# Weight preparation and early attention steps placed anew in a fused RetNet and leaky-ReLU kernel

## The chip, the cores and the metric

The kernel runs on one core of a Trainium2 chip. The metric is the device time of one execution in microseconds (us). The span of a trace, from the first to the last instruction, is about 2 us shorter than the time of the same execution. The granted clock is the share of TensorE's full clock that the profile shows. PE is TensorE, PEld its weight load, DVE is VectorE, ACT ScalarE, POOL GpSimd.

## The reference, cut to what matters

```python
# B, H, S, D = 4, 8, 768, 64
for t in range(S):
    state = gamma[None, :, None, None] * state + np.einsum('bhd,bhe->bhde', k[:, :, t], v[:, :, t])
    y[:, :, t] = scale * np.einsum('bhd,bhde->bhe', q[:, :, t], state)
x = y.transpose(0, 2, 1, 3).reshape(B * S, H * D)     # 3072 x 512
h = x @ w_in                                          # w_in 512 x 2048
g = np.maximum(0.01 * h, h)
return (g @ w_out).astype(np.float32)                 # w_out 2048 x 512
```

The data is fp32; the two weights are float64, so their eight-byte words reach the chip and are rounded to fp32 there.

## The kernel before

The sequence is cut into six chunks of 128 positions, c = 0 to 5. A chunk needs four **attention steps**, one for each batch entry b. A step is scores (`stage_a`: TensorE into two PSUM banks, VectorE multiplies by the mask), then the reading of scores and state (`yp`), an eviction into `x`, and the state update (`sp`). Two loops over the hidden dimension follow, in four units u of 512. The two matrix products of a unit are done by a scheme with seven products instead of eight, M1 to M7. I name one round of the seven a **call**: h(c,u) for the hidden layer, o(c,u) for the output.

```python
def seven(tiles, name, takes):
    which = [("M1", "A", 0, 0), ("M6", "B", 5, 5), ("M5", "C", 4, 4), ("M4", "D", 3, 6),
             ("M2", "A", 2, 2), ("M7", "B", 1, 1), ("M3", "C", 6, 3)]
    ...        # 4 matmuls each (8 records in the trace); PSUM bank A, B, C or D, tag "ff", 6 banks in all
        takes(m, ps)          # VectorE or ScalarE evicts and adds
        yield
```

The order matters for waits: M7 takes the bank that M6 filled, so M7 cannot start before VectorE has read M6 (into `u2`, in the trace `u`). M3 takes the bank of M5 in the same way (`m5`, in the trace `m`).

The weights come as 32 **pieces**, four for each of the eight blocks win[0..3] and wout[0..3]. One call of `round_piece` does this:

```python
def round_piece():
    n = done[0]; done[0] += 1
    if n == N_PIECES - 4:
        last.extend(work.tile(..., tag="raw", bufs=3, name=f"last{h}") for h in range(3))
    round_words(n)              # 3 ACTIVATEs on ScalarE (power of two of each word),
                                # then 3 operations on VectorE (mantissa, times power)
    ...                         # load of a later piece: three buffers "raw",
                                # and ONE buffer "raw_end" for the last four pieces
    if n % 4 == 3:
        sums(units[n // 4])     # 4 VectorE operations once a block is complete
```

Below, **powers** are the three ScalarE operations, **mantissas** the three VectorE operations, and **differences** are four VectorE operations on `x` (or `g`, giving `gd`) that play for activations the part that sums play for weights. The schedule of the first two chunks was this; steps inside a call are counted from 0, so `rounds(2, 4)` rounds one piece after the third product and one after the fifth:

```python
units = [win[0], wout[0], win[1], wout[1], win[2], win[3], wout[2], wout[3]]
for b in range(B):                       # chunk 0
    scored(0, b)(); round_piece(); read(0, b)()
differences(*xs[0])
run(hidden(0, *part[:1], *xs[0], *part[1:]), **rounds(2, 4))
for b in range(B):                       # chunk 1
    scored(1, b)()
    if b % 2 == 0:
        round_piece()
    read(1, b)()
differences(*xs[1])
for u in range(NU // 2):                 # units 0 and 1, each for both chunks
    for c in range(2):
        ...                              # hidden, rounds(2, 4)
    for c in range(2):
        run(output(c, os[c], [parts[c]], u == 0, False), **rounds(1, 3, 5))
for c in range(2):                       # units 2 and 3 as a pair, one output call for both
    ...
```

## Time and profile before

| | before |
|---|---|
| time, median (lowest to highest) | 735.77 us (734.89 to 736.97), 3 runs |
| span of the trace, mean granted clock | 734.1 us, 0.980 |
| TensorE busy / VectorE busy | 689.7 us (94%) / 365.1 us (50%) |
| VectorE operations | 579 |

The whole document uses one division of the span. It needs three lines of TensorE's timeline: the first product M1 of chunk 0, of chunk 1 and of chunk 2. The columns are start in us, duration, engine, source line, operation, tiles, shape and count.

```profile
28.08 1.99 PE L273 MATMUL A_h<-x,win 128*128 128x256 f32 x8
...
78.83 1.99 PE L273 MATMUL A_h<-x,win 128*128 128x256 f32 x8
...
297.01 1.89 PE L273 MATMUL A_h<-x,win 128*128 128x256 f32 x8
```

They cut the 734.1 us into an **opening** of 28.08, a **first stage** of 50.75 (one hidden call of chunk 0 and the attention of chunk 1), a **second stage** of 218.18 (the other 15 calls of the first two chunks with the rounding of 24 of the 32 pieces, and the attention of chunk 2) and a **rest** of 437.09 (chunks 2 to 5). The change rewrites the first three.

### The profile page before, as it was taken

Reading aid. Unit: us, or ns where it says so; the run is one execution under the profiler, and the core shown is the slowest. Engines: PE = TensorE matmul, PEld = TensorE weight load, DVE = VectorE, ACT = ScalarE, POOL = GpSimd, SP = SyncE. Lnnn points to the kernel's source line nnn. Section 1 sums busy time; section 2 is a strip of 40 time slices with the busy share of each in tenths; the row PEclk is TensorE's granted clock in tenths of the full one; section 3 lists DMA queues with packets and bytes.
Section 4 is the critical chain, followed back from the end, with each engine's and each line's share of the span. In section 5 each row is a group of like instructions: output and inputs, shape, how many; then the busy total and the mean of one; then the engine's idle time right before and its main releaser. Section 6 shows DMA issues by size and latency. Waiting matters only on the chain.

```text
span 734.1 us, 9584 instructions
## 1 busy us (share of the span) xinstructions
PE 689.7 (94%) x4096; PEld 594.2 (81%) x4096; DVE 365.1 (50%) x579; ACT 164.0 (22%) x273; POOL 26.2 (4%) x29
## 2 busy tenths in 40 slices
PE   5667999989779999999999999999999999999997
PEld 5556888877658888888888888888888888888886
DVE  4857598899654354351355253255243246251342
ACT  4050265463510120021011011111021021031210
POOL 1201100000000010000000000000000000000000
PEclk9888999999979999999999999999999999999999
DMA  8716223231202310220020120021121000100001
GB/s 303 256 58 225 92 94 137 86 104 68 87 0 100 131 58 14 81 78 1 29 87 1 61 92 21 0 80 36 58 65 51 0 2 0 58 1 0 2 1 58
DMA packets 15163, 49.12 MB, mean 67 GB/s; under 512 B 1680, under 2 KB 1680, under 8 KB 15120
## 3 DMA queue, kind: packets, MB, share of 16 engines
q1 hardware_dynamic: 15120, 48.51, 19.0%
q8 instruction: 32, 0.52, 0.3%
q14 instruction: 11, 0.09, 0.0%
HBM read 42.21 MB, written 6.29 MB: 66 GB/s over the span
## 4 chain that ended last, share of the span: by engine, by line
PE 83%; DVE 11%; ACT 2%; issue 2%; DMA 1%; SPq 0%; DVEq 0%
PE B_o L273 11%; PE B_h L273 11%; PE C_o L273 10%; PE C_h L273 10%; PE A_h L273 10%; PE A_o L273 10%; PE D_o L273 5%; PE D_h L273 5%; PE yp L147 3%; PE yp L142 3%; PE a0p L123 3%; DMA raw<-in_weights_dram 1%; PE sp L158 1%; ACT g L288 1%; PE a1p L123 1%
## 5 line engine op out<-in xcount | busy, mean ns | idle before, releaser
L273 PE MATMUL A_h<-x,win 128*128 128x256 f32 x384 | 91.2, 380 | 1.1 <-ACT m L293 1.1
L273 PEld LDWEIGHTS A_h<-x,win 128*128 128x128 f32 x384 | 72.5, 190 | 11.4 <-ACT m L293 1.5
L273 PE MATMUL A_o<-g,wout 128*128 128x256 f32 x288 | 69.8, 383 | 0.0
L288 ACT ACTIVATE g<-g 128x512 f32<-128x512 f32 x72 | 43.9, 630 | 105.3 <-DVE g L238 105.3
L273 PEld LDWEIGHTS A_o<-g,wout 128*128 128x128 f32 x288 | 55.1, 192 | 8.0 <-ACT m L330 0.4
L152 DVE TENSOR_TENSOR x<-yp,dec 128x512 f32<-128x512 f32 x24 | 16.6, 690 | 86.6 <-PE yp L147 86.6
L293 ACT COPY m<-A_h 128x512 f32<-128x512 f32 x24 | 14.0, 584 | 199.3 <-PE A_h L273 191.3
L273 PE MATMUL B_h<-t,win 128*128 128x256 f32 x192 | 47.6, 392 | 4.8 <-DVE t L241 4.8
L273 PE MATMUL B_h<-x,win 128*128 128x256 f32 x192 | 46.7, 386 | 0.9 <-DVE u L238 0.9
L273 PE MATMUL C_h<-t,win 128*128 128x256 f32 x192 | 47.4, 390 | 0.0
L273 PEld LDWEIGHTS B_h<-t,win 128*128 128x128 f32 x192 | 37.2, 196 | 11.0 <-DVE t L241 5.6
L273 PE MATMUL C_h<-x,win 128*128 128x256 f32 x192 | 45.4, 379 | 0.0
L273 PE MATMUL D_h<-t,win 128*128 128x256 f32 x192 | 45.4, 379 | 0.0
L112 POOL TENSOR_TENSOR kv<-kv,dec 128x512 f32<-128x512 f32 x24 | 25.7, 1072 | 528.6 <-DMA kv<-in_kv_dram 481.7
L238 DVE TENSOR_TENSOR m<-m,B_o 128x512 f32<-128x512 f32 x14 | 9.6, 685 | 68.8 <-PE B_o L273 68.8
L123 PE MATMUL a0p<-qk 64*128 64x128 f32 x192 | 31.3, 307 | 11.1 <-DVE x L152 6.4
L273 PEld LDWEIGHTS C_h<-t,win 128*128 128x128 f32 x192 | 36.2, 193 | 6.1
L273 PEld LDWEIGHTS B_h<-x,win 128*128 128x128 f32 x192 | 35.4, 190 | 6.8 <-DVE u L238 1.3
L273 PEld LDWEIGHTS C_h<-x,win 128*128 128x128 f32 x192 | 36.5, 190 | 5.0
L273 PEld LDWEIGHTS D_h<-t,win 128*128 128x128 f32 x192 | 36.5, 190 | 5.0
L123 PEld LDWEIGHTS a0p<-qk 64*128 64x128 f32 x192 | 26.1, 205 | 17.7 <-DVE x L152 7.0
L273 PE MATMUL C_o<-g,wout 128*128 128x256 f32 x144 | 34.7, 381 | 2.8 <-DVE m L238 2.8
(91 smaller groups left out, 1077.8 us busy)
## 6 DMA issues: line engine op xcount, KB each, us to landing
raw<-in_weights_dram SPq DMA_DIRECT2D x32, 512.0 KB, 3.2
qk<-in_qk_dram SPq DMA_DIRECT2D x24, 512.0 KB, 3.8
kv<-in_kv_dram SPq DMA_DIRECT2D x24, 512.0 KB, 4.4
out_dram<-o SPq DMA_DIRECT2D x24, 256.0 KB, 2.0
dec<-decay_dram SPq DMA_DIRECT2D x1, 262.0 KB, 5.4
```

What stands on the lines that cost most here:

```text
L112: nc.gpsimd.tensor_tensor(out=v, in0=v, in1=gk.unsqueeze(2).to_broadcast([128, H, D]), op=ALU.mult)
L123: nc.tensor.matmul(ps[j][:, a, :], lhsT=x[ts(j, 64), 1, a, :], rhs=x[ts(j, 64), 0, a, :])
L142: nc.tensor.matmul(yp[ts(j, 64), a, :], lhsT=st[b][ts(j, 64), a, :], rhs=x[ts(j, 64), 0, a, :], start=(a == 0), stop=False, skip_group_che ...
L147: nc.tensor.matmul(yp[ts(j, 64), a, :], lhsT=vs[:, 2 * a + j, :], rhs=am[j][:, a, :], start=(c == 0 and a == 0), stop=True, skip_group_che ...
L152: nc.vector.tensor_tensor(out=blocks, in0=yp.rearrange("p (kh k) t -> p kh k t", k=2), in1=gq.rearrange("p (kh k) t -> p kh k t", k=2), op ...
L158: nc.tensor.matmul(sp[ts(j, 64), a, :], lhsT=ks[:, 2 * a + j, :], rhs=vs[:, 2 * a + j, :], start=(a == 0), stop=True, skip_group_check=True)
L238: nc.vector.tensor_tensor(out=out, in0=a, in1=b, op=ALU.add)
L273: nc.tensor.matmul(ps[:, i, :], lhsT=block(w, sa)[:, k, ts(i, 128)], rhs=rhs[:, k, :], start=(first and i == 0 and n == 0 and k == 0), sto ...
L288: nc.scalar.activation(g[:, i], g[:, i], AF.Prelu, alpha=0.01)
L293: nc.scalar.copy(out=got["m1"], in_=ps)
```

## The change

The intent is to take away waits of TensorE for VectorE and ScalarE before chunk 2:

1. All four units go through the first two chunks one at a time, in the order win[0], wout[0], win[1], wout[1] and so on, so each block is needed when it arrives. There is no pair of units any more, which costs two more partial output calls.
2. ScalarE's powers run two pieces ahead of VectorE's mantissas.
3. The last four pieces lie in the four buffers of the attention inputs instead of in a single one.
4. Scores of chunk 0 and of steps 2 and 3 of chunk 1 use the six PSUM banks of the products.
5. Steps 0 and 1 of chunk 1 are woven into the first hidden call, whose products get another order.
6. The sums of win[0] alternate with the differences of chunk 0 instead of going before the last eviction of `x`.
7. In hidden calls rounding moves from steps 2 and 4 to 1 and 3, in output calls from 1, 3 and 5 to 1 and 4.

The diff, cut to its core (cuts are marked with `...`; the rest makes generators of `sums` and `differences`, and adapts helpers and the host's order of the pieces):

```diff
-    def stage_a(c, b):
+    def stage_a(c, b, banks="att"):
-        ps = [psum.tile([128, HP, C], FP32, tag="att", bufs=2, name=f"a{j}p_{c}_{b}")
+        ps = [psum.tile([128, HP, C], FP32, tag=banks, bufs=BANKS[banks], name=f"a{j}p_{c}_{b}")
...
-        if n < NC * B:
+        if n < NC * B and n - 2 * B not in range(AHEAD):
             load(*divmod(n, B))
...
-    units = [win[0], wout[0], win[1], wout[1], win[2], win[3], wout[2], wout[3]]
+    units = [w for pair in zip(win, wout) for w in pair]
...
-        raws[n] = work.tile([128, W], I64, tag="raw_end" if end else "raw", bufs=1 if end else 3,
-                            name=f"raw{n}")
+        tag, bufs = ("raw", 3) if n < N_PIECES - 4 else (("qk", "kv")[n % 2], AHEAD)
+        raws[n] = work.tile([128, W], I64, tag=tag, bufs=bufs, name=f"raw{n}")
...
-            round_words(n)
+            mantissas(n)
+        load_piece(n + 3)
+        if n + 2 < N_PIECES and f64:
+            powers(n + 2)
...
+        if n % 4 == 3 and n > 3:
+            all_of(sums(units[n // 4]))
...
-        scored(0, b)()
+        scored(0, b, banks="ff")()
         round_piece()
         read(0, b)()
-    differences(*xs[0])
+    all_of(differences(*xs[0]), sums(win[0]))
...
+    for u in range(NU):
+        parts = []
         for c in range(2):
+            parts.append(new_g(c, u))
+            order = {}
+            at = rounds(1, 3)
+            if (c, u) == (0, 0):
+                xs[1] = new_x(1)
+                order["order"] = ("M1", "M2", "M6", "M5", "M4", "M7", "M3")
+                at = put(rounds(1), s0=[scored(1, 0)], s2=[read(1, 0)], s3=[scored(1, 1)],
+                         s5=[read(1, 1)])
+            elif (c, u) == (1, 0):
+                for b in range(2, B):
+                    scored(1, b, banks="ff")()
+                    round_piece()
+                    read(1, b)()
+                differ(1)()
+                at = rounds(1)
+            elif (c, u) == (1, NU - 1) and NC > 2:
+                xs[2] = new_x(2)
+                at = put(at, s4=[scored(2, 0)], s6=[read(2, 0)])
+            run(hidden(c, u, *xs[c], *parts[c][1:], **order), at)
         for c in range(2):
...
+            at = rounds(1, 4) if u < NU - 1 else {}
+            if u == NU - 1 and NC > 2:
+                if c == 0:
+                    at = dict([(0, [scored(2, 1)]), (2, [read(2, 1)]), (3, [scored(2, 2)]),
+                               (5, [read(2, 2)])])
+                else:
+                    at = {0: [scored(2, 3)], 2: [read(2, 3)], 4: [differ(2)]}
+            run(output(c, os[c], [parts[c]], u == 0, u == NU - 1), at)
```

## The prediction

> **What bounds the kernel now.** I read the page first (strips and chain), then a table of stretches, then TensorE's timeline where it has gaps. From the page:
>
> ```profile
> PE   5667999989779999999999999999999999999997
> DVE  4857598899654354351355253255243246251342
> PEclk9888999999979999999999999999999999999999
> ...
> PE 83%; DVE 11%; ACT 2%; issue 2%; DMA 1%; SPq 0%; DVEq 0%
> ```
>
> A slice is 18.4 us. TensorE is full from the 13th slice on (220 us) to the last but one. Only the time before has room: TensorE is at 5 to 7 tenths in the first four slices and at 7 in the 11th and 12th, after VectorE ran at 8 or 9 for five slices, and the granted clock dips. The 11% of VectorE in the chain (some 80 us) must therefore lie there too. The table of stretches sizes it (stretch, its length, then busy us and counts by engine, clock, DMA share, GB/s):
>
> ```profile
> 0.00:28.00 28.00, 17.60 (x192) 15.35 (x192) 14.87 (x27) 8.90 (x13) 4.66 (x9) 1.00 0.86 306
> 28.00:79.00 51.00, 34.96 (x316) 29.77 (x315) 34.56 (x54) 10.87 (x18) 5.93 (x5) 0.83 0.40 139
> 79.00:147.00 68.00, 67.48 (x312) 58.94 (x312) 54.30 (x89) 37.12 (x63) 1.04 (x1) 1.00 0.31 107
> 147.00:205.00 58.00, 50.02 (x228) 41.37 (x227) 47.42 (x79) 29.08 (x49) 0.00 (x0) 0.97 0.23 82
> 205.00:241.00 36.00, 30.58 (x210) 25.48 (x209) 17.52 (x29) 1.10 (x2) 1.04 (x1) 0.91 0.17 59
> 297.00:410.00 113.00, 113.00 (x707) 97.70 (x706) 46.60 (x75) 17.30 (x29) 4.17 (x4) 1.00 0.14 48
> ```
>
> Idle TensorE: 10.4 us, 16.0, 0.5, 8.0 and 5.4 in the first five, 0 in the sixth. The timeline names what ended the longest gaps:
>
> ```profile
> 34.37 3.78 PE L273 MATMUL B_h<-t,win 128*128 128x256 f32 x8 [4.29 <-DVE t L241]
> ...
> 54.48 1.97 PE L142 MATMUL yp<-qk,st 64*64 64x128 f32 x16 [5.90 <-DVE am L128]
> ...
> 150.10 1.99 PE L273 MATMUL B_o<-g,wout 128*128 128x256 f32 x8 [0.92 <-DVE u L238]
> ...
> 167.29 1.99 PE L273 MATMUL C_o<-g,wout 128*128 128x256 f32 x8 [1.65 <-DVE m L238]
> ...
> 199.08 1.34 PE L273 MATMUL A_o<-g,last 128*128 128x256 f32 x4 [2.23 <-ACT g L303]
> ...
> 211.19 2.07 PE L273 MATMUL B_o<-gd,last 128*128 128x256 f32 x4 [5.42 <-DVE gd L241]
> ```
>
> Each is TensorE waiting for VectorE, or for ScalarE held up by a weight piece that arrived late. After the first gap eight matmuls took 3.78 us where they take 1.73 elsewhere: the clock was halved.
>
> **What the Trainium skill says.** "TensorE: Matmul & The Clock Gate", Back-to-back issue gap: N/2.4 + 2.5 ns when warm, 109 ns at N = 256. The trace has eight records of 216 ns for one fp32 product of eight (1.727 us), so it agrees if each fp32 matmul runs two passes per record. The same page, What's actually happening: about 3.4 us of idling halves the clock and about 3.4 us of work restores it. The trace agrees for the gaps of 4.29 and 5.42 us. "VectorE: DVE Perf Modes", The perf-mode tier table: fp32 tensor_tensor has only the 1x mode; the errata section of that page gives (N+151)/0.96, or 691 ns at 512. The trace has 681 to 692 ns, and starts 0.60 us apart when independent, 0.72 when the second reads the first. "Perfetto Trace Analysis", Matmuls: independent groups should rotate through different PSUM banks so that eviction overlaps. That is the intent of moving the early scores; the trace shows the wait it removes (scores of head group 1 started 1.21 us late, behind the x eviction of group 0).
>
> **The change part by part.** Dense costs first. A "call" (seven products of one unit) is 7 x 1.727 = 12.09 us of TensorE. One chunk in steady state, from the first product at 297.01 to the next chunk's at 409.69, is 112.68 us for eight calls (96.7), so an attention step costs (112.68 - 96.7)/4 = 4.0 us.
>
> *Opening, to the first product (28.08 us before).* Scores in six other banks let scores b+1 follow directly on step b; powers made early take ScalarE's part (three ACTIVATEs, 1.93 us) out of VectorE's waits. But the K/V tiles of steps 2 and 3 were waited for by GpSimd until 19.64 and 24.31 us, with DMA at 0.86. I move those by under 1 us, so the first product starts at about 27.8: gain nearly 0.
>
> *From the first product to the second chunk's first (28.08 to 78.83 us before, 50.75 us).* Dense it is one call and four attention steps: 12.1 + 16 = 28.1. Walking the new order with the 0.60 and 0.72 us spacings: the eight interleaved differences and sums end at about 33.0 (36.5 before); M1, scores, M2 fill TensorE until 32.3, when M6's operands are ready; two attention steps lie between products, so M3 ends at about 47.5. Then the second half of chunk 1 starts as badly as before: VectorE finishes g and gd at 51.9 and the score masks at 53.1, so TensorE idles about 4 us and probably halves its clock. Two steps of some 4 us follow; chunk 1's first product comes at about 61.5. Interval 33.7 instead of 50.75: gain 17. One weight piece and one set of sums (1.87 + 2.6 us of VectorE) is left over to the next stage.
>
> *From there to chunk 2's first product (78.83 to 297.01 before, 218.2 us).* Fifteen calls and four attention steps: 15 x 12.09 + 16 = 197.3 dense; the kernel before loses 20.9 here. What the change adds: outputs one unit at a time, so two more partial outputs, 2 x 9 VectorE operations, 18 x 0.69 = 12.4 us. Is VectorE enough? Per unit (two hidden and two output calls, 48.4 us of TensorE): hidden 2 x 6.5 (nine operations and a 0.7 us wait for ScalarE), output 2 x 5.9, eight pieces x 1.87 (0.46 + 0.80 + 0.61 from start to start), two sums x 2.6: 13 + 11.8 + 15 + 5.2 = 45.0. It fits, at 93%. Lags inside: rounds move from steps 2 and 4 to 1 and 3 and no longer wait for ScalarE, so the first operation of the output call ends at 6 us into it (9.9 before, at 149.36), where M7 needs it at 8.6; its m5 at 9.0, where M3 needs it at 10.4. So the waits of 0.92 to 1.65 us vanish, narrowly. The last pieces no longer share one buffer but use the chunk-input buffers: the 2.23 and 5.42 us gaps vanish, with their half clock. New: in the last unit scores of step 1 share two banks with step 0, whose eviction follows gd; I find TensorE waiting about 2 us there, and 0.5 at chunk 1's first differences, 2.5 and 0.5 with some clock. Gain 20.9 - 3.0 = 17.9.
>
> *After chunk 2's first product*: the same code, 436.9 us, gain 0.
>
> Sum: 0 + 17 + 17.9 = 35 us. 735.8 - 35 = 701.
>
> **Rivals.** (1) VectorE becomes the bound in the first two chunks. For: 93% by my count, and the trace has operations of 762 to 932 ns on average in some groups of sums, and waits for ScalarE's leaky step of 0.7 us each; before, it was 82% busy in 147 to 205 and already stalled TensorE. Against: 79 to 147 ran at 80% with 0.5 us lost. If each of three units overruns by 4 us, 713. (2) Opening and chunk 1 stay bound by arrivals and by the mask-evict-mask chain with the clock halved. For: the GpSimd waits at 19.64 and 24.31. Against: after 28 us the DMA share is 0.40. Half the 17 us would be lost: 709. (3) Powers placed ahead of evictions on ScalarE block them when a piece is late. For: in-order engine, waits up to 6.3 us for raw pieces at the start. Against: three buffers, 3.2 us to landing against some 6 us between rounds, and ScalarE needs 24 of 48.4 us per unit. Worth up to 5 us. (4) On the other side, no half clock in chunk 1 and a shorter wait there: about 696.
>
> **Range and chances.** Rivals 1 to 3 add, each unlikely in full, and together weigh more than rival 4; the floor with no stall in either part is 735.8 - 22.6 - 20.9 = 692. Range 692 to 712. Faster by 2% means under 721, which needs less than half the sum: 0.95. Within 2%: 0.04. Slower: 0.01.
>
> **What would show it.** Right: first product still near 28 us; chunk 1's first product near 61.5; chunk 2's near 262; no idle TensorE over 1 us between 62 and 240; VectorE above 90% there; a gap of about 4 us near 50 and one of 2 us in the last unit; about 437 us afterwards. Wrong: gaps of 1 us or more before M7 or M3 of output calls (rival 1); chunk 1's first product after 68 (rival 2); ScalarE waiting for raw pieces just before a gap (rival 3); any change after chunk 2's first product.

## The result, and the profile after

| | before | after |
|---|---|---|
| time, median (lowest to highest) | 735.80 us (734.89 to 736.97), 4 runs | 703.74 us (702.56 to 705.67), 4 runs |
| span of the trace, mean granted clock | 734.1 us, 0.980 | 701.8 us, 0.987 |

The ratio is 0.9566 with a 95% interval of 0.954 to 0.9592: faster by 4.3%. Here and below a ratio is the mean time of one kernel's fast runs over the mean of the other's in the same group of runs, so it is not quite the ratio of the medians. The predicted time was 701, the range 692 to 712.

The page of the kernel after, first the totals, then the strips and the chain of the work that ended last (a slice is 17.5 us):

```profile
PE 680.5 (97%) x4096; PEld 589.9 (84%) x4096; DVE 373.5 (53%) x597; ACT 166.9 (24%) x275; POOL 26.6 (4%) x29
...
PE   4898999999999999999999999999999999999997
...
DVE  4868767888889555512553442544351354341442
...
PEclk9799999999999999999999999999999999999999
...
PE 92%; DVE 4%; DMA 2%; ACT 1%; issue 0%; POOL 0%; SPq 0%; DVEq 0%; POOLq 0%
```

TensorE now reads 8 or 9 from the second slice to the last but one, and VectorE's share of the chain fell from 11% to 4%. VectorE has 597 operations instead of 579: 18 more, and still less of the time hangs on it. Its digits stay at 7 to 9 from the seventh slice to the 13th, so it is not idle; it is in time. The table of stretches, at the new boundaries, with the second stage split by unit (length, then busy us and counts of PE, PEld, DVE, ACT, POOL, then clock, DMA share, GB/s):

```profile
0.00:28.70 28.70, 17.79 (x193) 15.88 (x193) 15.94 (x28) 12.78 (x19) 5.74 (x10) 0.82 0.83 308
28.70:62.20 33.50, 29.88 (x314) 25.00 (x312) 25.89 (x45) 9.23 (x15) 3.86 (x4) 0.95 0.39 138
62.20:99.80 37.60, 36.57 (x171) 31.91 (x169) 29.07 (x49) 17.66 (x29) 0.00 (x0) 1.00 0.26 84
99.80:148.20 48.40, 48.40 (x226) 42.67 (x225) 38.84 (x64) 23.23 (x38) 0.00 (x0) 1.00 0.24 78
148.20:196.50 48.30, 48.30 (x226) 42.59 (x225) 41.92 (x69) 22.90 (x38) 0.00 (x0) 1.00 0.31 108
196.50:264.40 67.90, 66.47 (x482) 56.40 (x481) 48.55 (x79) 11.94 (x20) 6.54 (x6) 0.97 0.34 113
```

Units 1 and 2 (99.8 to 196.5) take 48.4 and 48.3 us with TensorE busy in all of it; four calls of 12.09 us make 48.4. In the kernel before, TensorE idled for 8 us in the stretch from 147 to 205 us, which holds the output calls of unit 1 and the hidden calls of units 2 and 3 of chunk 0. TensorE's timeline has these boundaries and these gaps (the number in brackets is the idle time just before, with what ended it):

```profile
17.27 0.37 PE L125 MATMUL a0p<-qk 64*128 64x128 f32 x1 [2.03 <-DMA qk<-in_qk_dram]
...
28.69 1.99 PE L301 MATMUL A_h<-x,win 128*128 128x256 f32 x8
...
54.62 1.71 PE L149 MATMUL yp<-am,kv 128*64 128x128 f32 x15 [3.48 <-issue]
...
62.25 1.99 PE L301 MATMUL A_h<-x,win 128*128 128x256 f32 x8
...
65.27 2.00 PE L301 MATMUL B_h<-t,win 128*128 128x256 f32 x8 [1.03 <-DVE t L253]
...
228.10 0.48 PE L125 MATMUL a0p<-qk 64*128 64x128 f32 x2 [1.43 <-DVE x L154]
229.51 3.42 PE L301 MATMUL B_o<-gd,last 128*128 128x256 f32 x8
232.72 2.19 PE L301 MATMUL C_o<-gd,last 128*128 128x256 f32 x8
...
264.44 1.89 PE L301 MATMUL A_h<-x,win 128*128 128x256 f32 x8
```

The gaps of 4.29, 5.90, 0.92, 1.65, 2.23 and 5.42 us that the prediction shows of the kernel before are gone. Three remain after the first product: 3.48, 1.03 and 1.43. The first is marked "issue", meaning the profile shows no releaser for it. VectorE's timeline does: the score masks are the last thing that these `yp` matmuls need.

```profile
51.18 2.14 DVE L253 TENSOR_TENSOR gd<-g,gd 128x512 f32<-128x512 f32 x2
53.24 0.68 DVE L253 TENSOR_TENSOR g<-g 128x512 f32<-128x512 f32 x1
53.84 0.68 DVE L130 TENSOR_TENSOR am<-a0p,mask 128x512 f32<-128x512 f32 x1
54.44 0.68 DVE L130 TENSOR_TENSOR am<-a1p,mask 128x512 f32<-128x512 f32 x1
```

The scores began on TensorE at 48.96, five us before; their masks stand behind `gd` in VectorE's order, and only the first mask was written when `yp` began at 54.62. This is a gap by order, not by lack of work. The stage table compared:

| us | opening | first stage | second stage | rest |
|---|---|---|---|---|
| before | 28.08 | 50.75 | 218.18 | 437.09 |
| after | 28.69 | 33.56 | 202.19 | 437.36 |
| gain | -0.61 | 17.19 | 15.99 | -0.27 |
| predicted gain | 0 | 17 | 17.9 | 0 |

The four gains sum to 32.3 us, as 734.1 - 701.8 does.

### The profile page after: what moved, and what is told of

Same layout as the page of the kernel before. It is cut to its first block, busy times and chain, and to the rows that moved or that the text cites. A ratio compares the mean times of both kernels' runs of the same rounds, so it can differ in the third digit from the quotient of the medians.

```text
span 701.8 us, 9573 instructions
## 1 busy us (share of the span) xinstructions
PE 680.5 (97%) x4096; PEld 589.9 (84%) x4096; DVE 373.5 (53%) x597; ACT 166.9 (24%) x275; POOL 26.6 (4%) x29
## 4 chain that ended last, share of the span: by engine, by line
PE 92%; DVE 4%; DMA 2%; ACT 1%; issue 0%; POOL 0%; SPq 0%; DVEq 0%; POOLq 0%
PE B_o L301 12%; PE C_o L301 12%; PE B_h L301 12%; PE A_o L301 12%; PE C_h L301 11%; PE A_h L301 11%; PE D_o L301 6%; PE D_h L301 6%; PE yp L149 4%; PE a0p L125 3%; PE yp L144 2%; PE sp L160 1%; DVE gd L253 1%; DMA qk<-in_qk_dram 1%; DMA dec<-decay_dram 1%; DVE am L130 1%
## 5 line engine op out<-in xcount | busy, mean ns | idle before, releaser
L301 PE MATMUL A_o<-g,wout 128*128 128x256 f32 x288 | 68.0, 379 | 0.0
L301 PE MATMUL B_h<-t,win 128*128 128x256 f32 x192 | 45.5, 380 | 1.0 <-DVE t L253 1.0
L250 DVE TENSOR_TENSOR m<-m,B_h 128x512 f32<-128x512 f32 x24 | 16.5, 686 | 45.4 <-PE B_h L301 45.4
L149 PE MATMUL yp<-am,kv 128*64 128x128 f32 x384 | 31.3, 299 | 7.9 <-issue 4.3
```

What stands on the lines that cost most here:

```text
L149: nc.tensor.matmul(yp[ts(j, 64), a, :], lhsT=vs[:, 2 * a + j, :], rhs=am[j][:, a, :], start=(c == 0 and a == 0), stop=True, skip_group_che ...
L250: nc.vector.tensor_tensor(out=out, in0=a, in1=b, op=ALU.add)
L301: nc.tensor.matmul(ps[:, i, :], lhsT=block(w, sa)[:, k, ts(i, 128)], rhs=rhs[:, k, :], start=(first and i == 0 and n == 0 and k == 0), sto ...
```

## The experiments

Twelve runs in three groups, each on one chip and compared with runs of the kernel before on that chip: e1 to e4 on chip 9 (median before 733.68 us, 7 runs), then a0, e5, b1 and b3 on chip 11 (735.33, 7 runs), then e6, s3, e7 and e8 on chip 9 again (734.01, the 7 runs of the first group and one more). Because these medians differ, I compare ratios; a difference of ratios times 735.8 us is told as a cost. An interval is about 0.003 to either side, so the difference of two ratios carries about 0.004, or 3 us, and a smaller one is not told apart from none. The stages come from one profile of each run. The last column of the table shows that in every run the rest of the kernel took 437.1 to 437.6 us: all differences arise before chunk 2. All outputs were correct.

| run | what differs from the kernel after | median us | ratio to before (95%) | opening | first stage | second stage | rest |
|---|---|---|---|---|---|---|---|
| after | | 703.74 | 0.9566 (0.954 to 0.9592) | 28.69 | 33.56 | 202.19 | 437.36 |
| a0_after | nothing | 703.33 | 0.957 (0.9549 to 0.9592) | 26.91 | 34.57 | 202.35 | 437.4 |
| e1_two_banks | part 4 undone | 705.18 | 0.9609 (0.9581 to 0.9638) | 29.76 | 35.68 | 200.26 | 437.3 |
| e2_no_lead | part 2 undone | 703.8 | 0.9596 (0.9573 to 0.962) | 26.25 | 34.76 | 202.96 | 437.3 |
| e3_one_end_buffer | part 3 undone | 708.91 | 0.9665 (0.9645 to 0.9686) | 26.22 | 34.66 | 208.37 | 437.2 |
| e4_pairs | part 1 undone | 707.86 | 0.9649 (0.9626 to 0.9672) | 26.47 | 34.22 | 206.57 | 437.5 |
| e5_chunk1_after | part 5 undone | 703.63 | 0.9579 (0.9547 to 0.9612) | 28.71 | 35.00 | 200.62 | 437.3 |
| e6_no_lead_late | parts 2 and 7 (hidden) undone | 712.46 | 0.9711 (0.9689 to 0.9733) | 30.07 | 33.48 | 210.23 | 437.3 |
| s3_extra | some 24 us of VectorE added | 724.97 | 0.9876 (0.985 to 0.9902) | 29.30 | 33.74 | 223.65 | 437.3 |
| e7_after_two_banks | parts 4 and 5 undone | 709.83 | 0.9666 (0.9633 to 0.9698) | 29.43 | 38.19 | 202.45 | 437.3 |
| e8_old_first_stage | parts 4, 5, 6 and early rounds undone | 716.23 | 0.9766 (0.9741 to 0.9792) | 29.42 | 47.76 | 200.06 | 437.6 |
| b1_scores_first | scores of steps 2 and 3 of chunk 1 earlier | 699.68 | 0.9523 (0.9498 to 0.9547) | 26.78 | 32.82 | 199.76 | 437.3 |
| b3_both | b1, and one more score in other banks | 697.83 | 0.949 (0.9467 to 0.9514) | 27.24 | 31.74 | 198.17 | 437.3 |

Two cautions. First, after, a0 and s3 run the same code up to the first product, and their openings are 28.69, 26.91 and 29.30 us, with a granted clock of 0.82, 1.00 and 0.83. So no difference under 2.5 us in the opening column is ascribed to any edit. The column does hint that the banks matter in it, which I had overlooked: at a clock of 0.94 or more, the runs with six banks (a0, e2, e3, e4, b1, b3) took 26.22 to 27.24 us, and those with two banks took 28.08 (before), 29.76 (e1), 29.43 (e7) and 29.42 (e8). This compares single profiles across runs, so it is not shown. Second, e1 and e5 have the second stage of the kernel after unchanged, and took 200.26 and 200.62 us for it against 202.19 and 202.35, mostly because no half clock followed the gap in the last unit there (the product after it took 1.99 us in both, and 3.42 and 3.59 in after and a0). So a difference of 2 us in that column can be the clock's.

My **theory**, beside the prediction: in the first stage, weaving attention into the hidden call gives most of the 17 us; in the second, the rounding order, the unit order and the buffers of the last pieces give the rest; and VectorE is nearly full but in time. The **rivals**: that it is the PSUM banks that matter in the first stage, that the lead of the powers matters in the second, or that VectorE is already the bound.

### The kernel after again

a0_after is the kernel after, run in the second group.

> The changed kernel unaltered, as the base for the runs beside it and to see how far its opening varies. In its first profile the clock was halved from 16 to 28 us and the first product came at 28.7 us; in three variants run on another chip the clock stayed whole and it came at 26.2 to 26.5. Theory: chance of the clock, so the ratio to before stays between 0.954 and 0.960 whichever way it falls.

The ratio is 0.957, next to 0.9566: the result holds in a second group of runs, in each stage to 1.8 us.

### First group: each part undone alone

**e1_two_banks** puts the early scores back into the two attention banks:

```diff
-        scored(0, b, banks="ff")()
+        scored(0, b)()
...
-                    scored(1, b, banks="ff")()
+                    scored(1, b)()
```

> Only the early scores go back to the two shared banks. Theory (the banks hardly matter, since the opening waits for inputs and the second half of chunk 1 waits for the masks): the opening moves by under 1 us, the second half of chunk 1 loses about 1 us because its first state products must now wait for the masks; in all 703 to 706 us. Rival (the other banks carry a good part of the 17 us): over 709 us.

The ratio, 0.9609, is some 0.004 or 3 us above that of the kernel after, about as large as the noise of the two together. The median is inside the 703 to 706 us expected. The first stage took 35.68 us, 1 to 2 us more, as expected; the opening took 29.76 us, against the expectation of no change over 1 us (see the first caution).

**e2_no_lead** computes the powers directly before the mantissas that need them:

```diff
         if f64:
+            powers(n)
             mantissas(n)
...
-        if n + 2 < N_PIECES and f64:
-            powers(n + 2)
```

> Only the lead of the powers is undone: the three ScalarE steps of a piece stand directly ahead of its VectorE steps again. Theory (the lead takes ScalarE's 1.93 us out of VectorE's way, but the earlier round places alone keep most of the lateness out): VectorE waits about 1 us in some rounds, some products before M7 and M3 wait, 706 to 710 us. Rival A (the lead is what removes the stalls of 147 to 205 us): 714 us or more. Rival B (it does nothing): 703 to 705 us.

0.9596, and a second stage of 202.96 us against 202.19 and 202.35: taken away alone, the lead costs 0 to 2 us, which is inside the noise. Rival B held; the 706 to 710 us of the theory did not come.

**e3_one_end_buffer** gives the last four pieces one buffer again, with the loads and powers in the old places:

```diff
-        tag, bufs = ("raw", 3) if n < N_PIECES - 4 else (("qk", "kv")[n % 2], AHEAD)
+        tag, bufs = ("raw", 3) if n < N_PIECES - 4 else ("raw_end", 1)
...
+            if n >= N_PIECES - 4:
+                powers(n)
             mantissas(n)
```

> Only the last four pieces go back to one buffer of their own, and chunk 2's inputs to their usual place. Theory: load, powers, mantissas and the next load follow each other again at 6.5 to 7 us a piece, the last sums come about 9 us late, and TensorE shows a gap of about 5 us in the last unit with a half clock after it; 711 to 714 us. Rival (the wait is hidden behind the dense products): 703 to 706 us.

0.9665, some 7 us more, of which 6 are in the second stage. The gap and the half clock came as expected; the time, 708.91 us, lies under the 711 to 714 expected. Its timelines of ScalarE, VectorE and TensorE near the last piece, in three fences:

```profile
220.81 0.66 ACT L233 ACTIVATE last<-raw 128x512 f32<-128x512 uint16 x1 [5.54 <-DMA raw<-in_weights_dram]
```

```profile
222.17 0.43 DVE L245 TENSOR_SCALAR last<-raw 128x512 uint32<-128x512 uint32 x1 [4.51 <-ACT z L235]
```

```profile
227.44 1.97 PE L144 MATMUL yp<-qk,st 64*64 64x128 f32 x16 [6.06 <-DVE am L130]
```

With one buffer the last piece cannot be loaded before the piece ahead of it is rounded. ScalarE waits 5.54 us for it, VectorE then 4.51 for ScalarE, and TensorE 6.06 for a mask that stands behind this piece and its sums in VectorE's order. A late load becomes a gap in the engine that sets the end, two engines further on. After the gap the matmuls of `yp` take 1.97 instead of 1.09 us.

**e4_pairs** takes units 2 and 3 as a pair again, with the old order of the blocks and the old rounds for it (the diff is in the main that part of the change, reversed):

```diff
-    units = [w for pair in zip(win, wout) for w in pair]
+    units = [win[0], wout[0], win[1], wout[1], win[2], win[3], wout[2], wout[3]]
...
-    for u in range(NU):
+    for u in range(NU // 2):
...
+    for c in range(2):
+        pair = []
+        for u in range(NU // 2, NU):
...
+        run(output(c, os[c], pair, False, True), at)
```

> Units 2 and 3 are taken as a pair after units 0 and 1, with weights in that order, as before; the lead, the banks, the buffers and the woven chunk 1 stay. It saves 2 x 9 VectorE operations (12.4 us) but wants all 32 pieces by about 171 us instead of 219. Theory (the order matters because VectorE then needs some 118 us of work in 109 us of TensorE's): stalls of 9 to 15 us in all, 711 to 719 us. Rival (the order is not needed once the powers come early): 702 to 706 us.

0.9649, some 6 us more, less than the 711 to 719 us of the theory and more than the 702 to 706 of the rival. TensorE has gaps again, first for `m`, then for `gd`:

```profile
148.45 2.15 PE L301 MATMUL C_o<-g,wout 128*128 128x256 f32 x5 [2.64 <-DVE m L250]
...
184.25 1.13 PE L301 MATMUL B_o<-gd,last 128*128 128x256 f32 x4 [2.35 <-DVE gd L253]
```

So the single units pay for their 18 added VectorE operations: with pairs there are fewer operations, but more of them fall into fewer calls of TensorE.

### Second group: weaving, and two attempts to do better

**e5_chunk1_after** undoes the weaving. All four attention steps of chunk 1 follow the first hidden call, which has the old order of products; scores stay in the six banks.

```diff
-                order["order"] = ("M1", "M2", "M6", "M5", "M4", "M7", "M3")
-                at = put(rounds(1), s0=[scored(1, 0)], s2=[read(1, 0)], s3=[scored(1, 1)],
-                         s5=[read(1, 1)])
+                at = rounds(1)
...
-                for b in range(2, B):
+                for b in range(B):
```

> Only the weaving is undone: the first call runs in its old order and all four attention steps of chunk 1 follow it, as before; the lead, the banks and the buffers stay. Theory (the weaving is most of the 17 us between the first product and chunk 1's first): 8 to 12 us over the changed kernel run beside it. Rival (the banks and the freed VectorE did it): under 4 us over.

0.9579, equal to a0 within the noise. **Here my theory fell**: weaving is not most of the 17 us. The trace says why:

```profile
47.71 2.30 PE L149 MATMUL yp<-am,kv 128*64 128x128 f32 x15 [3.02 <-issue]
...
52.12 1.09 PE L144 MATMUL yp<-qk,st 64*64 64x128 f32 x16
...
60.16 1.09 PE L144 MATMUL yp<-qk,st 64*64 64x128 f32 x16
```

The first step still waits 3.02 us. Between the two others lies one more, at 56.14: from there on the steps follow each other every 4.0 us without an idle gap before the state products of `yp`, because the scores of the next step run in other banks while this step is masked and evicted. A step that is dense by itself needs no call around it. My new theory: banks and weaving are substitutes, and only taking both away shows what they are worth. e7 below tests that.

**b1_scores_first** goes after the 3.48 us gap. Scores of step 2 are issued before the last product of the first hidden call, and those of step 3 directly after that call, so their masks are no longer followed by a mask, evict, mask chain; the two pieces rounded between those steps move to other calls.

```diff
-                at = put(rounds(1), s0=[scored(1, 0)], s2=[read(1, 0)], s3=[scored(1, 1)],
-                         s5=[read(1, 1)])
+                at = put(rounds(1), s0=[scored(1, 0)], s2=[read(1, 0)],
+                         s3=[scored(1, 1), round_piece],
+                         s5=[read(1, 1), scored(1, 2, banks="ff")])
...
-                for b in range(2, B):
-                    scored(1, b, banks="ff")()
-                    round_piece()
-                    read(1, b)()
+                scored(1, 3, banks="ff")()
+                read(1, 2)()
+                read(1, 3)()
                 differ(1)()
-                at = rounds(1)
+                at = rounds(1, 3)
```

> An addition: scores and masks of step 2 of chunk 1 are put ahead of the g differences of the first call, and one weight round into VectorE's idle time before M7. Theory (the 3.5 us gap and the half clock after it come from the masks standing behind g and gd on VectorE): chunk 1's first product comes 3 to 5 us earlier and the whole is 3 to 5 us under the changed kernel. Rival (VectorE's own work is the limit of that stage): within 1 us of it.

0.9523 against a0's 0.957: some 3.5 us less (the runs do not overlap: 698.44 to 700.62 against 702.87 to 704.44 us). The total came as expected, but not where I expected it. A gap stays in the first stage, now for the eviction of step 2, which stands behind the same `gd` and the masks of step 3:

```profile
55.96 1.09 PE L144 MATMUL yp<-qk,st 64*64 64x128 f32 x16 [3.29 <-DVE x L154]
```

The first stage is only 1.8 us shorter than in a0, and chunk 1's first product comes 1.9 us earlier instead of 3 to 5. The other 2.6 us lie in the second stage: the gap of 1.03 us at its start is gone, and no half clock followed the gap of 1.33 us in the last unit, which by the second caution can be chance. So the theory of the masks is not shown by this run.

**b3_both** is b1 with one more score step of chunk 2 in the six banks, against the 1.43 us gap at 228.10 us:

```diff
-                    at = dict([(0, [scored(2, 1)]), (2, [read(2, 1)]), (3, [scored(2, 2)]),
+                    at = dict([(0, [scored(2, 1, banks="ff")]), (2, [read(2, 1)]), (3, [scored(2, 2)]),
```

> The previous addition, and the scores of step 1 of chunk 2 in the six other banks. Theory (the 1.43 us gap at 228 us and the half clock after it, 3.42 and 2.19 us for two products of 1.73, come from the two shared banks): a further 2.5 to 4 us, so 6 to 9 us under the changed kernel, and faster than both kernels. Rival (the gap moves to the next wait for the same VectorE work): under 1.5 us further.

0.949, a median of 697.83 us: this version beats both kernels, the one after by 0.8%. Against b1 it is 2.4 us less, within the noise; the gap in the last unit is gone, as its lines show. Its stretches of the first and second stage, then TensorE's timeline:

```profile
27.20:59.00 31.80, 27.76 (x317) 23.32 (x313) 27.03 (x44) 8.91 (x15) 4.28 (x4) 1.00 0.44 153
59.00:257.10 198.10, 197.58 (x1098) 171.87 (x1097) 159.20 (x259) 77.44 (x128) 6.39 (x6) 1.00 0.29 100
```

```profile
56.47 1.09 PE L144 MATMUL yp<-qk,st 64*64 64x128 f32 x16 [3.21 <-DVE x L154]
58.98 1.99 PE L301 MATMUL A_h<-x,win 128*128 128x256 f32 x8
...
223.90 1.99 PE L301 MATMUL B_o<-gd,last 128*128 128x256 f32 x8
...
257.15 1.89 PE L301 MATMUL A_h<-x,win 128*128 128x256 f32 x8
```

The second stage is at 198.17 us, 0.9 above the dense 197.3, and the clock is whole in both. A gap of 3.21 us is left in the first stage.

### Third group: what two parts are worth together, and how full VectorE is

**e6_no_lead_late** undoes the lead as e2 does, and moves the rounds of hidden calls back to steps 2 and 4:

```diff
-            at = rounds(1, 3)
+            at = rounds(2, 4)
```

> The lead undone and, with it, the rounds of the hidden calls put back to their old places (after the third and fifth product). Theory (early places and lead are each enough alone; only without both are the mantissas late): VectorE waits 1 to 2 us a round, the first operation of an output call ends past 8.6 us into it, TensorE waits before M7 and M3 in two or three units; 3 to 7 us over the changed kernel. Rival (neither matters, VectorE has room enough): within 1.5 us of it.

0.9711: 10 us more than the kernel after, of which 8 in the second stage, where I had expected 3 to 7 in all. The gaps of the kernel before are back, at M7 and M3 of the output calls, and two in the last unit:

```profile
135.75 1.99 PE L300 MATMUL B_o<-g,wout 128*128 128x256 f32 x8 [0.52 <-DVE u L249]
...
138.93 1.99 PE L300 MATMUL C_o<-g,wout 128*128 128x256 f32 x8 [1.19 <-DVE m L249]
...
231.96 1.09 PE L144 MATMUL yp<-qk,st 64*64 64x128 f32 x16 [2.40 <-DVE am L130]
...
239.12 0.48 PE L125 MATMUL a0p<-qk 64*128 64x128 f32 x2 [2.65 <-DVE x L154]
```

Together with e2 this says that with rounds in the early places the lead is worth nearly nothing, and without both some 10 us is lost. The fourth corner, late rounds with the lead, was not run, so late rounds alone may cost as much.

**s3_extra** repeats a difference in six hidden calls and the addition into `m5` in six output calls, three times each. The repeated operations write the same values again, so the result stays right. That is 36 operations of 0.68 us, some 24 us of VectorE in the second stage.

```diff
                 leaky(1)
+                if c < 2 and u > 0:
+                    for _ in range(3):
+                        minus(gd[:, 0], g[:, 1], g[:, 0])
                 all_of(differences(g, gd))
...
-                    plus(got["m5"], o[:, 3], ps)
+                    for _ in range(1 + 3 * (c < 2)):
+                        plus(got["m5"], o[:, 3], ps)
```

> A gauge: three repeated VectorE operations (the first g difference, the m5 sum) in each hidden and output call of units 1 to 3 of the first two chunks, results unchanged: 12 x 0.62 to 0.72, some 8 us a unit. By my count VectorE then needs 53 of 48.4 us in units 1 and 2. Theory (VectorE is within some 3 us a unit of being the bound): 4 to 10 us over the changed kernel. Rival (much more room than counted): under 1 us over.

0.9876: 22.5 us more, where I had expected 4 to 10. Nearly all that was added lands in the time:

```profile
191.84 2.51 PE L301 MATMUL B_o<-g,wout 128*128 128x256 f32 x8 [2.20 <-DVE u L250]
...
197.12 3.40 PE L301 MATMUL C_o<-g,wout 128*128 128x256 f32 x8 [2.77 <-DVE m L250]
...
250.01 0.58 PE L125 MATMUL a0p<-qk 64*128 64x128 f32 x1 [5.90 <-DVE x L154]
```

The idle us of VectorE are where it waits for a product or for ScalarE, and work put in front of an operation that TensorE needs delays it all the same. Units 1 and 2 took 55.4 and 56.3 us instead of 48.4, and VectorE was busy for 45.7 and 50.2 us of them: it did not run full. The run put its operations directly in front of ones that TensorE waits for, so it shows how little slack their order has; it does not show that VectorE's time is used up. The same work in other places was not tried.

**e7_after_two_banks** undoes banks and weaving together, e1 and e5 in one:

```diff
-        scored(0, b, banks="ff")()
+        scored(0, b)()
...
-                order["order"] = ("M1", "M2", "M6", "M5", "M4", "M7", "M3")
+                at = rounds(1)
...
-                for b in range(2, B):
-                    scored(1, b, banks="ff")()
+                for b in range(B):
+                    scored(1, b)()
```

> Chunk 1 unwoven and the early scores in the two shared banks. New theory (weaving and free banks each let TensorE run ahead of VectorE, so that one stands in for the other; without both, each step waits for the eviction of the step before): the steps of chunk 1 take 5 us again instead of 4.0; with the opening 5 to 9 us over the changed kernel. Rival (neither matters, the 17 us come from elsewhere): under 4 us over.

0.9666, or 7 us over the kernel after, inside the 5 to 9 expected, where the two alone cost 3 and 0.7. The first stage is 38.19 us. The steps are 5.0 us apart instead of 4.0, and each `yp` waits for a mask:

```profile
55.10 1.09 PE L144 MATMUL yp<-qk,st 64*64 64x128 f32 x16 [0.58 <-DVE am L130]
...
65.11 1.09 PE L144 MATMUL yp<-qk,st 64*64 64x128 f32 x16 [0.58 <-DVE am L130]
```

The new theory held in sign: banks and weaving seem to replace each other in part. It is weakly supported, since the runs with both in place took 33.48 to 34.76 us for this stage, e1 35.68, e5 35.00 and e7 38.19: e7 lost less than 2 us beyond the sum of the two. In size, the stage lost about 4 us, a quarter of 17, so most of the 17 was still unaccounted for.

**e8_old_first_stage** therefore also puts the sums back behind every fourth piece, before the last eviction of chunk 0, and the rounds of the first call and of chunk 1 into their old places:

```diff
-        if n % 4 == 3 and n > 3:
+        if n % 4 == 3:
...
-    all_of(differences(*xs[0]), sums(win[0]))
+    differ(0)()
...
+                at = rounds(2, 4)           # first hidden call
...
+                    if b % 2 == 0:          # chunk 1
+                        round_piece()
```

> As the run before, and in addition the sums of the first weights stand ahead of the last x eviction and of the differences again, and the second weights' rounds and sums inside chunk 1 as before; only the lead stays. New theory (what is left of the 17 us is VectorE order: sums ahead of work that TensorE waits for): the stretch from the first product to chunk 1's first takes 46 to 50 us again, 11 to 16 us over the changed kernel. Rival (it was the lead): within 6 us.

The first stage is 47.76 us, nearly the 50.75 of the kernel before, and the time is 14 us up, both as expected. The table of stretches for the first stage and TensorE's timeline in it:

```profile
29.40:77.20 47.80, 35.66 (x314) 30.51 (x313) 33.34 (x53) 10.99 (x18) 4.97 (x4) 0.82 0.35 120
```

```profile
34.51 3.44 PE L301 MATMUL B_h<-t,win 128*128 128x256 f32 x8 [2.50 <-DVE t L253]
...
51.67 1.97 PE L144 MATMUL yp<-qk,st 64*64 64x128 f32 x16 [3.99 <-DVE am L130]
...
70.46 0.48 PE L125 MATMUL a0p<-qk 64*128 64x128 f32 x2 [3.78 <-DVE x L154]
```

The gaps at 34.51 and 70.46 us are sums standing in VectorE's order ahead of an eviction of `x`, the first those of win[0], the second those of wout[0]. The gap at 51.67 us is of the kind that the kernel after has too, masks behind `gd`. With these gaps the granted clock of the stage is 0.82, where the kernel after has 0.95. Some of what the kernel after saves here is only moved: it rounds one piece and does one set of sums fewer in this stage. Whether that costs it anything later is not shown: e8's second stage took 200.06 us against 202.19, but e1 and e5, with nothing moved, took 200.26 and 200.62. How the 9.6 us between e7 and e8 divide among sums, rounds and clock was not run, and stays open.

## Why the prediction was right, point by point

- **Opening, gain nearly 0: right.** The first product came at 28.69 us, in the second run at 26.91, against 27.8 predicted; runs of the same code scatter by as much, and in a0, whose clock was whole here as in the kernel before, the gain was 1.2 us. The 2.03 us gap at 17.27 us ends with a load of `qk`: arrivals still set a part of it.
- **First stage, 33.7 us: right to 0.2 us** (33.56; 34.57 in a0). The gap of about 4 us "near 50" came as 3.48 us at 54.62: VectorE was done with the masks 2 us later than I had walked it. The half clock after it came too (15 matmuls of `yp` took 1.71 us, where 16 take 1.09). The term was right as a whole, and e5 shows that I had the wrong part as its cause: I took the weaving to be most of it. The walk gave a sum for the new order as a whole, and its success does not speak for that belief. By e8 the new places of sums, rounds, banks and weaving together make 14.2 of the 17.2 us (47.76 against 33.56); how they share it stays open.
- **Second stage, gain 17.9: off by 1.9 us, and this is most of the 2.7 us by which the sum was too high** (35 predicted, 32.3 measured). The mechanism was right: one gap in chunk 1's first differences, one in the last unit, the other waits gone. The mis-sized term is the loss that stays, "2.5 and 0.5 with some clock", that is 3.0. It measured 202.19 - 197.3 = 4.9: a gap of 1.03 instead of 0.5; a gap of 1.43 with half clock after it, during which B_o and C_o took 3.42 and 2.19 us instead of 1.73 each, 2.15 more, together 3.6 instead of 2.5; and 0.3 elsewhere. The half clock was in part bad luck (second caution). b3, without the two gaps of over 1 us and without half clock, took 198.17. Of the signs named, chunk 2's first product came at 264.44 instead of near 262, and "no idle TensorE over 1 us between 62 and 240" was missed by the gap of 1.03 us; the gap in the last unit lies in that stretch too, so the prediction had contradicted itself there.
- **VectorE fits, at 93%: right in what follows, too high in the number.** I counted 45.0 us in a unit; in units 1 and 2 VectorE was busy for 38.84 and 41.92 us, or 80 and 87%. From 62.2 to 240 us it was busy for 143.5 of 177.8, or 81%, so the sign "above 90%" did not come. The 18 added operations were counted right (597 against 579), but VectorE's busy time rose by 8.4 us, not 12.4: some operations took less time (the groups of sums at 932 and 762 ns before are at 692 and 685), and operations close behind each other overlap in the record.
- **Waits before M7 and M3 vanish, because `u` ends its wait at 6 us into the output call and `m5` at 9.0: right.** In a0 the M1 of output call o(0,1) began at 123.31 us, and VectorE's two operations are these:

```profile
128.60 0.68 DVE L250 TENSOR_TENSOR u<-m,B_o 128x512 f32<-128x512 f32 x1
...
131.71 0.68 DVE L250 TENSOR_TENSOR m<-o,C_o 128x512 f32<-128x512 f32 x1
```

They end 129.28 - 123.31 = 6.0 and 132.39 - 123.31 = 9.1 us into the call, before the 8.6 and 10.4 at which M7 and M3 want them. I called this narrow. e2 and e6 say that it bears the loss of the lead (0 to 2 us), and is used up without the lead and with late rounds (10 us).
- **Last pieces in four buffers: right.** e3 brings back a 6.06 us gap and 7 us of time. The kernel before lost 2.23 and 5.42 there.
- **The rest, gain 0: right**, 437.36 against 437.09 (the 436.9 in the prediction is a slip).
- **Rivals.** Rival 1, VectorE as the bound, did not happen; s3 shows how little more can stand in front of what TensorE waits for. Rival 2, no gain in chunk 1, fell with 62.25 us. Rival 3, ScalarE blocked by late pieces: it waited up to 6.3 us for a piece between 62 and 240 us, and no gap of TensorE followed. Rival 4, no half clock in chunk 1 and a shorter wait, did not happen either: both came. b3 reached 697.83 us, near its 696, but it is another kernel, and 4.2 us of its gain over a0 lie in the second stage.
- **Two readings in the prediction.** The 216 ns of a matmul record are twice the 109 that it sets beside them, and no run here shows why. The return of the clock agrees less well than it says: after the gaps of 4.29 and 5.42 us TensorE worked for some 5.1 and 5.7 us at half clock (0.50 from 34 to 38 us and 0.64 from 38 to 40; 0.50 from 212 to 216 and 0.77 from 216 to 218), not 3.4.

For the second stage the parts add up fairly well: undone alone or in a pair that covers for each other, the end buffers cost 6.2 us of it, the order of units 4.4, and lead with early rounds 8.0 (against 202.19); that is 18.6 where 16.0 was gained. Each figure can be off by some 2 us, by the second caution.

## What to carry to other kernels

Where an engine that works in program order, as VectorE does here, feeds the one that sets the end, put the operation that the other waits for first, and work that is needed later (here sums and weight rounding) behind it; the same operations, and even 18 more of them, can then cost less. Undo the parts of a change singly and together before saying what each is worth: the banks and the weaving cost 3 and 0.7 us alone, and 7 together. The busy share of an engine does not tell how much it can still take: VectorE was busy for 80 to 87% of a unit, and work put in front of operations that TensorE waits for landed almost whole in the time.

## What the Trainium skill lacked or had wrong

- "TensorE: Matmul & The Clock Gate", What's actually happening, ties the half clock to an idle window of some 3.4 us. Here shorter gaps were sometimes enough: in the last unit, at the same place in the code, gaps of 1.43 us (after), 1.59 (a0) and 1.69 (e2) were followed by a B_o of 3.42, 3.59 and 3.56 us, while gaps of 1.33 (b1), 1.55 (e5) and even 2.65 us (e6) left it at 1.99. The section does say that the window runs freely and so that its moment varies; what decides between these runs is not shown by them. In the kernel after, the gap of 1.43 us cost 2.15 us more than itself.
- "VectorE: DVE Perf Modes", The DRAIN you can't avoid, says that the next operation waits for the pipeline and that some start earlier, and gives no distance to an operation that reads the result of the one before it. That distance is 0.72 us for 128x512 operations of 0.68 to 0.69 us (`gd` at 125.94 and 126.66 us in a0), and independent ones start 0.60 us apart (the masks at 53.84 and 54.44 us).
- No page says how much a VectorE that is busy most of the time can still take. The run s3_extra gave one number: some 24 us, added in front of operations that TensorE waits for while VectorE was busy for 80 to 87% of a unit, cost 22.5 us.
